# 70 small zero products on TensorE in the kernel generation, and its side jobs placed anew

## The chip, the core and the metric

The kernel runs on one core of a Trainium2 chip. A core has five engines that each take their instructions in order: TensorE (PE in the profile; its weight loads are PEld), VectorE (DVE), ScalarE (ACT), GpSimd (POOL) and SyncE (SP, which here only starts transfers). Each has its own queue, and they wait for each other by semaphores. The metric is the device time of one execution in microseconds. Of the kernel before three runs are given: median 993.96 us, from 993.62 to 994.17.

## What is computed

One block of a network with two halves, both modulated by a condition vector. The first half is a long convolution: for each of 640 channels a kernel of 2048 samples is generated from 192 complex exponentials and applied by FFT. The second is a bilinear feed-forward network. B = 1, L = 2048, D = 640, N = 192, F = 1536, all f32.

```python
logdA = dt * A;  dB = dt * Bc
P = jnp.exp(logdA[:, :, None] * l[None, None, :])
K = jnp.einsum("dn,dnl,dn->dl", Cc, P, dB).real      # the kernel sums
y = irfft(rfft(pad(u)) * rfft(pad(K)))[:L] + u * Dskip
...
mod = silu(c) @ w_mod                                 # sa, ca, ga, sb, cb, gb
h = layernorm(x) * (1 + ca) + sa
x = x + ga * conv(h)
h = layernorm(x) * (1 + cb) + sb
x = x + gb * (((h @ w_gate) * (h @ w_up)) @ w_down)
```

## The kernel before

**Generation and convolution, to about 446 us.** The 640 channels are five blocks (`db`) of 128. A block has eight kernel sums, so `n` runs from 0 to 39, and a loop of 144 turns `t` has three turns for each `n`. For one `n`, POOL multiplies out three tables (`Ph`, angles; `EQ` and `EP`, magnitudes; L710), ACT takes their sines (`trig`, into the PSUM tiles `tra`/`trb`), DVE multiplies sines and magnitudes into `QtA`, `PtA`, `QtB`, `PtB` (L765 to L792), and PE adds the products of these up in one PSUM tile `kg` (L807 and L822, 32 products each; line L811 adds the skip term). One `kg` tile serves two `n`; ACT then copies it out as `Kt`.

**Side jobs.** Everything else of the first half runs between these turns: `u_seeds` (the starting values of a block's tables, much of it DVE work in one go), `tab_ph` and `tab_eq` (table doublings on POOL), `u_k`, `u_pre`, `u_g`, `u_c`, `u_d` (the FFT of the kernel, the FFT of the input, their product and the way back, on PE, DVE and ACT; between the stages data goes through DRAM buffers such as `hm`, `FH`, `WD`), the modulation rows (L360), statistics of the inputs. `u_d` reads `WD` into a tile `TV` (L959), transforms it (L967) and adds the input (L971, L974). `row_stats` and `u_fold` stand among them too.

**What sets the order.** Nothing is scheduled at run time. The dictionary `SCHED` holds a number for each step of each side job; in turn `t` the loop runs the steps whose number, divided by 10, is `2t` or `2t + 1`, in the order of the numbers. Numbers from 2400 on come after the last kernel sum. So `SCHED` writes each engine's instruction order. `SLOT` gives, for each ring of buffers, the letter (`a`, `b`, `c`) that each new tile takes, in turn; a new tile waits until the last reader of that letter is done.

```python
def due(x):
    for _, g in sorted(jobs.pop(x, []), key=lambda j: j[0]):
        next(g, None)
```

**The passage and the second half.** After the generation the last block is transformed back. `raw` (L1000) loads raw gate weights into `wga0` and `wga1` in turn, `split_g` splits them in a high and a low part (ACT, then DVE at L1022), and `u_head` takes the statistics of the first two groups of 512 tokens (L1130), normalizes, transposes (L1160) and starts the first feed-forward products (L1197). All loads and stores of this passage that SP starts stand in one queue. `warm` adds 30 and 4 small products to a scratch tile there. From 552 us on the feed-forward network runs with its own fixed order; the change doesn't touch it.

Of the kernel before, what the change touches and what calls it, by code (L numbers as in the profile page):

```python
# [18 lines left out]
P = 128  # L19
# [9 lines left out]
TURN = float(np.float32(2.0 * math.pi / 2.0**32 * (1.0 - 1.5e-7)))  # L29

SCHED = dict(
    ml=(-885, -929, -989),
    mr=(((98, 154), (90, 130)), ((-884, 78), (-877, 73)), ((-885, -881), (-889, 132))),
    st=(
        (-955, 11),
        (-929, 195),
        (-874, 149),
        (-925, 128),
        (-938, 121),
        (-879, 152),  # L40
        (-869, 167),
        (-924, 162),
        (-995, -925),
        (-938, -871),
        (-885, 93),
        (-990, -871),
        (50, 180),
        (51, 214),
        (-930, -878),
        (-927, 39),  # L50
    ),
    hm=(
        (120, 388),
        (119, 390),
        (123, 234),
        (-949, 306),
        (-1000, 254),
        (112, 246),
        (231, 293),
        (-871, 309),  # L60
        (266, 333),
        (324, 384),
        (315, 372),
        (134, 256),
        (463, 511),
        (335, 429),
        (391, 541),
        (479, 545),
    ),
    rstd=(228, 229),  # L70
    tab=(487, 829),
    fo=(157, 189, 197, 222),
    e0=(138,),
    ds=(205, 222, 503, 397),
    mc=((-872, 289, 307, 356, 356), (217, 378, 439, 446, 461), (309, 570, 620)),
    q=(
# [4 lines left out]
    ),  # L81
    pre=(
# [5 lines left out]
    ),  # L88
    c=(
# [5 lines left out]
    ),  # L95
    d=(
# [5 lines left out]
    ),  # L102
    k=(
        (189, 202),
        (208, 226),
        (356, 358),
        (499, 559),
        (422, 496),
        (634, 660),
        (663, 672),  # L110
        (698, 713),
        (672, 682),
        (820, 837),
        (947, 972),
        (1036, 1059),
        (915, 955),
        (956, 984),
        (1080, 1094),
        (1072, 1079),
        (1271, 1275),  # L120
        (1209, 1209),
        (1528, 1540),
        (1546, 1546),
        (1406, 1429),
        (1384, 1393),
        (1533, 1569),
        (1521, 1521),
        (1684, 1715),
        (1706, 1716),
        (1931, 1933),  # L130
        (1939, 1951),
        (1911, 1915),
        (2069, 2083),
        (2033, 2056),
        (1997, 2004),
        (2286, 2306),
        (2108, 2128),
        (2368, 2376),
        (2349, 2373),
        (2504, 2534),  # L140
        (2413, 2437),
        (2492, 2495),
        (2495, 2507),
    ),
    low=((145, 411, 641, 885, 1122, 1398, 1592, 1847, 2073), (209, 434, 680, 929, 1150, 1398, 1612, 1868, 2112)),
    w=(2508, 2575, 2790, 2776, 2819, 2829),
    wl=(2444, 2450),
    wm=(2801, 2834),
    h=(2480, 2716, 2875, 2876, 2878, 2878, 2878, 2878),
    g=(  # L150
# [5 lines left out]
    ),  # L156
)

SLOT = dict(
    Kt="abababaababbbabaabab",  # L160
    Ph="abababababababababababababababababababab",
    PtA="abababababababababababababababababababab",
    TV="ababbabaababababababababababaabbaabaaababababa",
    W="abbababababababababababab",
    f16="abababa",
    gh="abcaacbabcbcbcbacbacabccabcacbabcabc",
    hf="abcabcabcabcabcabcacabcabcacacacabababacacbcbabacbacbababcbcabcab",
    psf="abcabbaaccacbabcabacbcbcabcababcbcacabcaaabcbcabcaacacacabcabcabcacbcbacbacbaacbacbacbacbbacbaccbacbacbacbaacbacbaccacab"
    "cacabcabcabccabcabcabcabcabacbacbacbacbacbacbcabcababccabcabcaabcabcabcabcabcabccabcabcabcabcabcabcabcabccacbacbbabcabca"
    "bcacabcabcabcabcabcabcabcabcabc",  # L170
    tr="abababababababababababababababababababababababababababababababababababababababababababababababababababababababababababab"
    "a",
    xs="ababababababababbbab",
)
SEG0 = ("l", "a", "b", "c", "ud", "r", "x", "e", "f", "G", "g", "D", "h", "v", "R", "")
SEG = ("l", "a", "b", "c", "ud", "D", "r", "R", "x", "eE", "f", "g", "h", "v")
# [48 lines left out]
def tile_kernel(ctx: ExitStack, tc: tile.TileContext, I, out):  # L225
    nc = tc.nc
    V, S, G, PE, SY = nc.vector, nc.scalar, nc.gpsimd, nc.tensor, nc.sync
# [15 lines left out]
    ident = const.tile([P, P], F32, name="ident")  # L243
# [26 lines left out]
    def need(n, *k):  # L270

        assert done.get(k, 0) >= n, k
# [17 lines left out]
    f16 = fft.enter_context(tc.tile_pool(name="f16", bufs=2, side="right"))  # L290
# [7 lines left out]
    ct = kconst.tile([P, 800], F32, name="ct")  # L298
# [497 lines left out]
    kg_of = {}  # L796
# [118 lines left out]
    def u_c(db, qd, parts=1):  # L915

        k0, dn = 8 * qd, P // parts
        for d0 in range(0, P, dn):
# [354 lines left out]
    at(T0["fo"], u_fold)  # L1273
    at(T0["e0"], once(lambda: LATE.pop()()))
    for j in range(4):
# [570 lines left out]
```

## Time and profile before

| | us |
|---|---|
| median of three runs (lowest, highest) | 993.96 (993.62, 994.17) |
| the profiled execution | 996.15 |
| its span, first to last instruction | 994.4 |
| its mean granted TensorE clock | 0.95 |
| PE, DVE, ACT, POOL busy in the span | 893.7, 729.1, 577.0, 510.8 |
| generation and convolution | 24 to 446 |
| passage | 446 to 552 |
| feed-forward network | 552 to 994 |

How to read the rows that the prediction quotes. A row of stretches has: from and to, length, busy time and count of PE, PEld, DVE, ACT and POOL, the clock granted to TensorE (1.00 is full), the busy share of the DMA engines, GB/s. A row of the timeline has start, length, engine, line, operation, output and inputs, tile, shape and count, and in brackets the idle time before it and what ended it. An f32 product appears as two rows on PE, so "x10" are five products and "x64" are 32. A row of waits names the engine and the line that waited, the instruction that ended it, the total, how often, and the longest. The chain of waits is followed back from the last instruction; asked for a stretch, it gives the shares by line.

### The profile page before, as it was taken

The page shows a single profiled execution, that of the slowest core. Times are in us where ns is not written, and L with a number is a line of the kernel's source. Part 1 is how long each engine was busy: PE and PEld are TensorE (multiplying, and loading weights), DVE is VectorE, ACT ScalarE, POOL GpSimd, SP SyncE. Part 2 cuts the span into 40 slices and gives each one's busy share as a digit, 9 for nine tenths or more (in the row PEclk, how much of TensorE's full clock was granted, in tenths as well). Part 3 has the DMA queues.
Part 4 walks back from the last instruction along what each step waited for, and adds up shares of the span by engine and source line. Part 5 has one row for each costly group of instructions (what it writes and reads, how often), then busy time and mean ns, then how long its engine had stood idle before and what let it go on. Part 6 is the DMA issues. An engine that isn't in the chain of part 4 may idle for free.

```text
span 994.4 us, 26747 instructions
## 1 busy us (share of the span) xinstructions
PE 893.7 (90%) x11120; PEld 725.3 (73%) x11120; DVE 729.1 (73%) x1408; ACT 577.0 (58%) x1071; POOL 510.8 (51%) x400
## 2 busy tenths in 40 slices
PE   4867898899889689998877999999999999999998
PEld 3565656676576567777635888889999788888998
DVE  8798569889989887894758655566677656568952
ACT  4869989886978878772345333334455443435430
POOL 5978899799779989950030254440113122222110
PEclk9877889899889889999999899999999999999999
DMA  8728654555246443667685565724564577658875
GB/s 262 257 54 303 219 186 136 177 167 173 77 153 194 138 123 121 188 214 236 208 230 202 172 214 187 238 92 147 155 241 114 193 228 236 217 181 290 238 239 186
DMA packets 159337, 188.54 MB, mean 190 GB/s; under 512 B 10352, under 2 KB 128880, under 8 KB 158064
## 3 DMA queue, kind: packets, MB, share of 16 engines
q1 hardware_dynamic: 150000, 155.51, 48.8%
q0 software_dynamic: 4752, 21.63, 7.5%
q10 hardware_dynamic: 4464, 9.70, 2.6%
q8 instruction: 87, 1.43, 0.6%
q14 instruction: 34, 0.28, 0.1%
HBM read 124.22 MB, written 62.59 MB: 188 GB/s over the span
## 4 chain that ended last, share of the span: by engine, by line
PE 55%; DVE 14%; ACT 12%; issue 10%; DMA 6%; POOL 2%; SPq 1%; DVEq 0%; POOLq 0%; ACTq 0%
PE pa L1074 17%; PE pa L1508 9%; PE psg L1074 8%; PE psfc L889 2%; PE kg L822 2%; PE kg L807 2%; PE psfa L889 2%; ACT L230 1%; PE psfb L889 1%; ACT trb L230 1%; DMA TVa<-WD 1%; PE psfb L946 1%; PE pa L1560 1%; ACT tra L230 1%; PE psfc L946 1%
## 5 line engine op out<-in xcount | busy, mean ns | idle before, releaser
L1051 POOL TENSOR_TENSOR tf<-wur,wgb 128x256 f32<-128x256 f32 x23 | 18.2, 792 | 251.7 <-DVE wtl L1022 204.5
L710 POOL TENSOR_TENSOR EQ<-LQ,RH 128x1536 f32<-128x1536 f32 x40 | 124.2, 3105 | 9.8 <-DVE QtB L767 9.6
L1022 DVE TENSOR_TENSOR wtl<-tf,wth 128x256 fp32r<-128x256 f32 (+1 forms) x72 | 36.6, 509 | 58.9 <-ACT wth L230 58.9
L710 POOL TENSOR_TENSOR Phb<-LH,DH 128x1536 int32<-128x1536 int32 x20 | 62.3, 3114 | 13.5 <-ACT tra L230 13.5
L710 POOL TENSOR_TENSOR EP<-LP,RH 128x768 f32<-128x768 f32 x40 | 66.0, 1651 | 0.0
L710 POOL TENSOR_TENSOR Pha<-LH,DH 128x1536 int32<-128x1536 int32 (+1 forms) x21 | 62.4, 2971 | 2.9 <-ACT trb L230 2.6
L1508 PE MATMUL pa<-wsg,sh 128*128 128x384 f32 (+1 forms) x304 | 58.6, 311 | 0.0
L822 PE MATMUL kg<-QtB,PtB 64*32 64x64 f32 x2560 | 48.5, 229 | 5.9 <-DVE QtB L766 5.3
L822 PEld LDWEIGHTS kg<-QtB,PtB 64*32 64x32 f32 x2560 | 41.5, 114 | 16.0 <-issue 7.1
L1508 PEld LDWEIGHTS pa<-wsg,sh 128*128 128x128 f32 x304 | 45.8, 189 | 0.0
L1547 POOL DMA_DIRECT2D wsg<-wdc x21 | 11.2, 532 | 66.5 <-PE pa L1560 35.5
L1022 DVE TENSOR_TENSOR wsg<-wga,wsg 128x640 fp32r<-128x640 f32 x36 | 32.9, 920 | 11.9 <-ACT wsg L230 11.9
L1074 PE MATMUL pa<-sh,wth 128*128 128x512 f32 x112 | 35.3, 397 | 6.5 <-DVE a L1423 6.1
L1022 DVE TENSOR_TENSOR sl<-a,sh 128x512 fp32r<-128x512 f32 x53 | 36.7, 712 | 5.8 <-ACT sh L230 5.8
L230 ACT ACTIVATE sh<-a 128x512 fp32r<-128x512 f32 x53 | 32.0, 622 | 14.9 <-PE psg L1560 6.2
L230 ACT ACTIVATE a<-pa 128x512 f32<-128x512 f32 x12 | 7.2, 597 | 54.7 <-PE pa L1074 54.7
L230 ACT ACTIVATE wsg<-wga 128x640 fp32r<-128x640 f32 x36 | 26.1, 729 | 21.7 <-PE pa L1508 11.0
L230 ACT ACTIVATE wth<-tf 128x256 fp32r<-128x256 f32 (+1 forms) x72 | 32.2, 479 | 9.8 <-PE pa L1074 5.3
L1074 PE MATMUL pa<-hh,wsg 128*128 128x512 f32 x136 | 36.7, 395 | 0.5 <-DVE wsg L1022 0.5
L1139 POOL TENSOR_SCALAR hfa<-xb,hr,hr 128x128 f32<-128x128 f32 x4 | 2.3, 572 | 67.6 <-DVE hr L283 67.6
L230 ACT ACTIVATE s<-pa 128x512 f32<-128x512 f32 x11 | 6.6, 598 | 49.4 <-PE pa L1074 49.4
L765 DVE TENSOR_TENSOR QtA<-tra,EQ 128x1024 f32<-128x1024 f32 x20 | 24.4, 1221 | 14.8 <-PE kg L807 9.2
(665 smaller groups left out, 3143.8 us busy)
## 6 DMA issues: line engine op xcount, KB each, us to landing
wsg<-wdc POOLq DMA_DIRECT2D x21, 640.0 KB, 5.1
wgb<-B_w_gate SPq DMA_DIRECT2D x24, 320.0 KB, 4.7
wur<-B_w_up SPq DMA_DIRECT2D x24, 320.0 KB, 6.0
wsd<-wsg SPq DMA_DIRECT2D x12, 640.0 KB, 3.9
wga<-wdg SPq DMA_DIRECT2D x12, 640.0 KB, 4.6
wsg<-wsd POOLq DMA_DIRECT2D x12, 640.0 KB, 4.7
wdc<-xb SPq DMA_DIRECT2D x21, 320.0 KB, 4.2
TVb<-WD SPq DMA_DIRECT2D x22, 256.0 KB, 3.5
```

Source lines behind the costliest of these rows:

```text
L230: return S.activation(o, i, f, **kw)
L710: G.tensor_tensor(o.rearrange("p x (h l) -> p x h l", l=8), lo.unsqueeze(2).to_broadcast([P, rows, nh, 8]), hi.rearrange("p h x -> p x h") ...
L765: return [lambda: V.tensor_tensor(Qt[:, :, :, 0:32], tr[:, :, :, ::-1], e[:, :, 0:32].unsqueeze(1).to_broadcast([P, 2, R, 32]), op=OP.mult ...
L807: PE.matmul(kg[j * 32 : j * 32 + 32, dd, :], PtA[:, c, dl * 4 + j, :], QtA[:, c, dl * 4 + j, :], start=dd == 0 and c == 0, stop=False, til ...
L822: PE.matmul(kg[j * 32 : j * 32 + 32, dd, :], PtB[lo : lo + 64, c, r, :], QtB[lo : lo + 64, c, r, :], start=False, stop=dd == 7 and c == 1, ...
L889: PE.matmul(r[c][par * 64 : par * 64 + 64, i, :], t_tw[:, k0 + k, c, :], src[:, k, :], start=True, stop=True, tile_position=(0, par * 64))
L946: PE.matmul(r[par][:, i], t_ti[lo : lo + 64, qd * 4 + i, c, :], x[lo : lo + 64, c, i, :], start=c == 0, stop=c == 1, tile_position=(lo, 0))
L1022: V.tensor_tensor(lo, v, hi, op=OP.subtract)
L1051: E.tensor_tensor(t[:, 0:2], u[:, 0:2], g[:, 0:2], op=OP.subtract)
L1074: PE.matmul(ps, w[a][:, k], x[b][:, l], start=first and n == 0 and m == 0, stop=n == 2 and m == len(ks) - 1, skip_group_check=True)
L1508: PE.matmul(AC[tb][t][c], x[:, ts], w[:, cs], start=st, stop=f == NF - 1 and n == 2 and (c == 0 or t % 2 == 1))
L1547: G.dma_start(WD[q], wdc[:, q // 3, q % 3])
```

## The change

A new job `fill` puts two products on PE. Its weights are a 64x64 corner of the identity beside the diagonal, all zeros, its moving operand 64 rows of 256 columns of a table; the result, zeros, is added to columns of the newest `kg` tile. It is called at 70 places, set by a new list `fl` in `SCHED`. All other numbers of `SCHED` in the generation and passage and the letters of `SLOT` are different too; the loop and the jobs are not. Beside the 140 products on PE, ACT has four more loads of function tables (28 for 24); DVE, POOL and SP have as many instructions as before. Of these tables a line or two is shown.

```diff
 SCHED = dict(
+    fl=(
+        358,
+        189,
...
+        2282,
+        1873,
+    ),
-    ml=(-885, -929, -989),
+    ml=(-887, -915, -977),
...
-    w=(2508, 2575, 2790, 2776, 2819, 2829),
+    w=(2453, 2558, 2624, 2678, 2865, 2688),
...
-    h=(2480, 2716, 2875, 2876, 2878, 2878, 2878, 2878),
+    h=(2626, 2738, 2749, 2789, 2845, 2851, 2863, 2877),
...
 SLOT = dict(
-    Kt="abababaababbbabaabab",
+    Kt="abaabababaababababab",
...
+    def fill():
+
+        for _ in range(2):
+            PE.matmul(kg_of[max(kg_of)][0:64, 0:4], ident[0:64, 64:P], ct[0:64, 0:256].rearrange("p (d m) -> p d m", m=64), start=False, stop=False)
+
...
+    for v in T0["fl"]:
+        at((v,), once(fill))
```

Four places in the order of the instructions. A row has line, operation, output and inputs, shape and count; the lines of the changed kernel are 77 higher (84 after `fill`), so L822 is L899, L889 is L966, L1022 is L1099.

PE before, at the burst of seeds for the last block (340 us in the profile): two kernel sums with a transform between, then the transform of an input.

```order
L526 MATMUL psfa<-ct,prm 128x8x16
L527 MATMUL psfa<-ct,prm 64x8x8
L528 MATMUL psfa<-ct,prm 64x8x8
L807 MATMUL kg<-QtA,PtAa 32x64 x32
L967 MATMUL psfb<-TVb,ct 32x512 x4
L822 MATMUL kg<-QtB,PtB 32x64 x32
L889 MATMUL psfa<-ghb,t_tw 64x128 x2
L889 MATMUL psfb<-ghb,t_tw 64x128 x2
```

PE now, at the burst of seeds for the last block; L1314 are the new products.

```order
L884 MATMUL kg<-QtA,PtAa 32x64 x32
L1314 MATMUL kg<-ct,ident 64x256 x6
L603 MATMUL psfc<-ct,prm 128x8x16
L604 MATMUL psfc<-ct,prm 64x8x8
L605 MATMUL psfc<-ct,prm 64x8x8
L603 MATMUL psfc<-ct,prm 128x8x16
L604 MATMUL psfc<-ct,prm 64x8x8
L605 MATMUL psfc<-ct,prm 64x8x8
L899 MATMUL kg<-QtB,PtB 32x64 x32
L1314 MATMUL kg<-ct,ident 64x256 x14
L966 MATMUL psfa<-f16b,t_tw 64x128 x2
L966 MATMUL psfc<-f16b,t_tw 64x128 x2
```

Six zero products stand ahead of the seeds' small products and fourteen ahead of a transform, each behind a kernel sum; a transform of the kernel follows in place of one of the input. Over the whole program the new products stand at 43 places: 29 of two, 9 of four, 3 of six and 2 of fourteen products.

ACT before, at the square roots of the row statistics (`ry<-rv`): both stand side by side.

```order
L230 ACTIVATE f16b<-psfb 128x32x16
L230 ACT_TABLE_LOAD
L230 ACTIVATE ry<-rv 128x6
L230 ACTIVATE ry<-rv 128x10
L230 ACTIVATE f16a<-f16a,nm_95,rs_94 128x640
L230 ACTIVATE PtAa<-Pha 128x1024
L230 ACT_TABLE_LOAD
```

ACT now, at the first of the two.

```order
L307 ACTIVATE TVa<-psfa 1x384
L307 ACT_TABLE_LOAD
L307 ACTIVATE ry<-rv 128x6
L307 ACT_TABLE_LOAD
L307 ACTIVATE tra<-Pha 128x512
```

The second one stands further on, with a table load of its own ahead of it and one behind.

DVE before, in the passage (484 us in the profile): the last product of transforms, the statistics, the low parts of the gate weights, then the last additions.

```order
L936 TENSOR_TENSOR f16a<-TVa,psfc 128x4x64
L1130 BN_STATS a_7256<-xb_6905 128x6 x16
L1130 BN_STATS a_7257<-xb_6906 128x6 x16
L1022 TENSOR_TENSOR wsg<-wga_7039,wsg 128x640 x2
L1022 TENSOR_TENSOR wsg<-wga_7120,wsg 128x640 x2
L974 TENSOR_TENSOR xsa<-psfb,xsa 128x512
L971 TENSOR_TENSOR xb_6905<-psfc,xsb 128x4x128
```

DVE now, at the same point of the passage.

```order
L1013 TENSOR_TENSOR f16a<-TVb,psfa 128x4x64
L1099 TENSOR_TENSOR wsg<-wga_7089,wsg 128x640
L1099 TENSOR_TENSOR wsg<-wga_7207,wsg 128x640
L1051 TENSOR_TENSOR xsb<-psfc,xsb 128x512
L1051 TENSOR_TENSOR xsa<-psfc,xsa 128x512
L1207 BN_STATS a_7499<-xb_7045 128x6 x16
L1207 BN_STATS a_7500<-xb_7046 128x6 x16
L1048 TENSOR_TENSOR xb_7045<-psfb,xsb 128x4x128
```

The low parts stand ahead of the 32 statistics, and so does one more addition; one low part has moved up among the transforms and one further back.

SP now, in the passage: the load of raw weights into the buffer that the low parts free, and behind it the loads of the transformed data. Before, the same load stood directly ahead of the load of `TVa`.

```order
L1036 DMA TVa<-WD 128x4x128 x2
L1038 DMA xsa<-A_u 128x4x128
L1077 DMA wga_7412<-B_w_gate 128x5x256
L1052 DMA x2d<-xsb 128x4x128
L1036 DMA TVb<-WD 128x4x128 x2
```

A store of a sum stands between the two now.

More of the change, by code (lines that the diff above doesn't have):

```diff
@@ L31 @@
 SCHED = dict(
-    ml=(-885, -929, -989),
-    mr=(((98, 154), (90, 130)), ((-884, 78), (-877, 73)), ((-885, -881), (-889, 132))),
-    st=(
[L35 to L50, printed above, removed]
-    ),
-    hm=(
[L53 to L68, printed above, removed]
-    ),
@@ L70 @@
[L70 to L75, printed above, removed]
-    q=(
[4 rows of a table removed]
+    fl=(
+        358,
+        189,
+        377,
+        347,
+        553,
+        317,
+        309,
+        784,
+        132,
+        90,
+        718,
+        803,
+        432,
+        709,
+        791,
+        353,
+        306,
+        370,
+        668,
+        364,
+        1281,
+        116,
+        341,
+        1157,
+        127,
+        1334,
+        1625,
+        2252,
+        1781,
+        1301,
+        2146,
+        792,
+        801,
+        2052,
+        1779,
+        326,
+        1291,
+        2052,
+        1312,
+        327,
+        1638,
+        576,
+        112,
+        1793,
+        1278,
+        1332,
+        835,
+        1766,
+        1914,
+        1558,
+        2133,
+        1765,
+        1045,
+        1269,
+        1809,
+        357,
+        1629,
+        1674,
+        1742,
+        1743,
+        1806,
+        1786,
+        1750,
+        371,
+        1785,
+        2359,
+        1773,
+        1322,
+        2282,
+        1873,
+    ),
@@ new lines @@
+    ml=(-887, -915, -977),
+    mr=(((102, 122), (102, 109)), ((-863, 86), (-886, 53)), ((-887, -872), (-887, 27))),
+    st=(
+        (-1001, 0),
+        (-975, 121),
+        (-895, 54),
+        (-993, 48),
+        (-921, 45),
+        (-906, 63),
+        (-862, 97),
+        (-870, 79),
+        (-1007, -958),
+        (-989, -919),
+        (-899, 16),
+        (-930, -867),
+        (9, 117),
+        (118, 138),
+        (-1004, -933),
+        (-947, 2),
+    ),
+    hm=(
+        (7, 398),
+        (124, 443),
+        (129, 145),
+        (-910, 267),
+        (-871, 187),
+        (146, 162),
+        (231, 259),
+        (-875, 316),
+        (287, 339),
+        (315, 380),
+        (341, 376),
+        (104, 236),
+        (470, 515),
+        (421, 468),
+        (486, 543),
+        (425, 549),
+    ),
@@ L81 @@
+    rstd=(122, 193),
+    tab=(664, 769),
+    fo=(192, 199, 221, 259),
+    e0=(66,),
+    ds=(385, 254, 475, 495),
+    mc=((-862, 143, 202, 317, 364), (195, 454, 514, 529, 549), (323, 406, 412)),
+    q=(
[4 rows of a table added]
     ),
     pre=(
[5 rows of a table removed]
-    ),
-    c=(
[5 rows of a table removed]
-    ),
-    d=(
[5 rows of a table removed]
-    ),
-    k=(
[L104 to L143, printed above, removed]
-    ),
@@ L145 @@
-    low=((145, 411, 641, 885, 1122, 1398, 1592, 1847, 2073), (209, 434, 680, 929, 1150, 1398, 1612, 1868, 2112)),
-    w=(2508, 2575, 2790, 2776, 2819, 2829),
-    wl=(2444, 2450),
-    wm=(2801, 2834),
-    h=(2480, 2716, 2875, 2876, 2878, 2878, 2878, 2878),
-    g=(
[5 rows of a table removed]
[5 rows of a table added]
+    ),
+    c=(
[4 rows of a table added]
+        (
+            (2342, 2573, 2595, 2608, 2609, 2672),
+            (2434, 2461, 2569, 2576, 2602, 2667),
+            (2604, 2630, 2645, 2646, 2690, 2696),
+            (2431, 2536, 2539, 2562, 2579, 2649),
+        ),
+    ),
@@ new lines @@
+    d=(
[5 rows of a table added]
+    ),
+    k=(
+        (186, 190),
+        (188, 193),
+        (473, 493),
+        (530, 563),
+        (415, 431),
+        (481, 530),
+        (617, 625),
+        (686, 705),
+        (641, 668),
+        (690, 716),
+        (789, 826),
+        (839, 878),
+        (895, 901),
+        (941, 961),
+        (1058, 1076),
+        (1042, 1062),
+        (1411, 1423),
+        (1353, 1371),
+        (1245, 1265),
+        (1287, 1308),
+        (1475, 1497),
+        (1398, 1418),
+        (1545, 1573),
+        (1516, 1522),
+        (1661, 1666),
+        (1735, 1736),
+        (1814, 1836),
+        (1905, 1914),
+        (1847, 1862),
+        (2005, 2007),
+        (2010, 2016),
+        (1976, 1989),
+        (2139, 2171),
+        (2106, 2112),
+        (2304, 2324),
+        (2242, 2251),
+        (2450, 2511),
+        (2320, 2330),
+        (2447, 2503),
+        (2480, 2536),
+    ),
@@ L156 @@
+    low=((143, 433, 676, 914, 1138, 1371, 1597, 1876, 2098), (213, 427, 690, 891, 1165, 1364, 1602, 1852, 2114)),
+    w=(2453, 2558, 2624, 2678, 2865, 2688),
+    wl=(2453, 2532),
+    wm=(2706, 2789),
+    h=(2626, 2738, 2749, 2789, 2845, 2851, 2863, 2877),
+    g=(
[5 rows of a table added]
     ),
@@ L159 @@
 SLOT = dict(
-    Kt="abababaababbbabaabab",
+    f16="abababa",
+    TV="ababbabababbababababaabababababbbaaababbababab",
+    gh="abcabcbacacaacabcbacacbabcacbcaacbac",
+    psf="abcabbacbacbcacaabcbcbabcabcabcabacacbabacbacbacbacccababababcababcabcabcabcabcaabcabacbacbbacbacbacbacbacbacbacbacbbcbc"
+    "abcabcabcabcabbcabcabcabcabcabacbacacbabcbcabccabacacacbcabcabcccabcabbcabcabcabcabcaabcababcabcabbcabcabbcacacacabcabca"
+    "bcabcacbabacbacbacbacbacbacbaca",
     Ph="abababababababababababababababababababab",
-    PtA="abababababababababababababababababababab",
-    TV="ababbabaababababababababababaabbaabaaababababa",
     W="abbababababababababababab",
[L165 to L170, printed above, removed]
     tr="abababababababababababababababababababababababababababababababababababababababababababababababababababababababababababab"
     "a",
-    xs="ababababababababbbab",
+    PtA="abababababababababababababababababababab",
+    Kt="abaabababaababababab",
+    hf="abcabcbcababcbcabcabcacababcabcababacacbcbcbcacacacacacacacabcabc",
+    xs="abababababababababab",
 )
```

47 rows, old and new, of tables (c, d, g, pre) are left out of this document.

## The prediction

> **What bounds the kernel now.** I read the page from the top, then three stages, then the granted clock and the chain of waits inside the first stage.
>
> ```profile
> span 994.4 us, 26747 instructions
> PE 893.7 (90%) x11120; PEld 725.3 (73%) x11120; DVE 729.1 (73%) x1408; ACT 577.0 (58%) x1071; POOL 510.8 (51%) x400
> ...
> PEclk9877889899889889999999899999999999999999
> ...
> PE 55%; DVE 14%; ACT 12%; issue 10%; DMA 6%; POOL 2%; SPq 1%; DVEq 0%; POOLq 0%; ACTq 0%
> ...
> 24.00:446.00 422.00, 361.94 (x7812) 270.15 (x7814) 355.50 (x633) 349.94 (x639) 371.89 (x222) 0.89 0.54 169
> 446.00:552.00 106.00, 84.20 (x961) 60.80 (x954) 71.54 (x180) 43.11 (x81) 9.26 (x15) 0.97 0.70 220
> 552.00:994.40 442.40, 437.53 (x2316) 387.04 (x2315) 282.02 (x511) 171.92 (x328) 117.23 (x138) 1.00 0.61 198
> ```
>
> The last three rows give, for each stage, the busy time of PE, PEld, DVE, ACT and POOL, then the granted clock. From 552 us PE is busy 437.5 of 442.4 us at full clock: that stage has nothing for this change and moves as one block. In the generation (24 to 446 us) no engine is full, four are near it: PE 362, DVE 356, ACT 350, POOL 372 of 422 us. PE stands idle there 422 − 361.9 = 60 us, and its clock is 0.89. The clock comes in whole stretches of one half, thirteen of them:
>
> ```profile
> 36.71:43.54 6.83, 6.28 (x74) 5.18 (x75) 6.79 (x14) 5.02 (x8) 6.83 (x4) 0.50 0.59 206
> ...
> 343.91:354.15 10.24, 4.87 (x72) 4.18 (x76) 10.07 (x17) 10.18 (x26) 4.29 (x3) 0.50 0.30 89
> sum 92.14, PE 76.39 PEld 61.47 DVE 75.17 ACT 80.01 POOL 70.93; mean PE 5.88 PEld 4.73 DVE 5.78 ACT 6.15 POOL 5.46
> ...
> 125.46:128.87 3.41, 2.43 (x20) 0.59 (x16) 2.14 (x5) 3.38 (x7) 3.41 (x2) 1.00 0.94 331
> 128.87:132.28 3.41, 3.41 (x72) 1.70 (x65) 0.00 (x0) 3.38 (x6) 3.41 (x2) 0.50 0.79 259
> ...
> 340.50:343.91 3.41, 0.00 (x0) 0.00 (x0) 3.41 (x10) 3.33 (x6) 3.41 (x2) 1.00 0.97 271
> 343.91:347.32 3.41, 0.00 (x0) 0.00 (x0) 3.41 (x6) 3.40 (x11) 2.52 (x2) 0.50 0.63 185
> ```
>
> 92 us pass at half clock, 76 of them with PE busy. The lower rows are neighbouring windows of 3.41 us: after one with PE busy only 2.43 us, and after one with PE wholly idle, the next runs at 0.50. What half clock does to a product, and what the added products should cost, stands in four groups (start, length):
>
> ```profile
> 114.30 2.42 PE L360 MATMUL psfb<-t_tw,sil 128*128 128x256 f32 x10
> 116.66 1.10 PE L822 MATMUL kg<-QtB,PtB 64*32 64x64 f32 x64
> ...
> 109.18 1.10 PE L822 MATMUL kg<-QtB,PtB 64*32 64x64 f32 x64
> ...
> 132.31 1.93 PE L822 MATMUL kg<-QtB,PtB 64*32 64x64 f32 x64
> ```
>
> The same kernel sum takes 1.10 us warm and 1.93 us in the stretch at 128.87.
>
> **Term 1, the clock.** Only cold PE time on the chain can shorten the run. The chain of waits, asked for single stretches, gives shares by line (a piece that crosses an edge counts whole, so a row can pass 100%):
>
> ```profile
> by line: PE psfc L360 65.6%; PE kg L822 30.0%; DVE QtB L765 10.0%; DVE QtB L766 5.0%; issue 0.6%
> ...
> by line: PE kg L807 27.3%; PE kg L822 27.3%; PE psfb L424 25.5%; PE psfc L868 25.3%; PE psfa L868 0.7%
> ...
> by line: PE psfc L889 54.8%; PE psfa L889 37.5%; PE kg L807 13.5%
> ...
> by line: PE psfa L889 57.9%; PE psfc L889 37.5%; ACT hfc L230 14.5%; PE kg L807 6.0%; issue 1.3%
> ...
> by line: PE psfa L844 57.2%; PE psfb L889 25.0%; PE psfc L889 23.8%
> ...
> by line: PE psfb L946 53.4%; PE psfb L868 21.9%; PE kg L822 17.6%; PE psfc L946 11.9%; PE psfa L868 0.8%
> ...
> by line: DVE st L473 19.6%; PE kg L822 13.6%; PE psfc L403 12.5%; PE psfb L403 5.8%; issue 5.4%; DVE mv L474 5.0%; DVE PtB L792 4.7%; DVE QtB L765 4.4%; PE psfb L404 3.1%; PE psfb L844 3.0%; DVE psfb L550 2.8%; DVE pta L549 2.7%; DVE prm L5
> ...
> by line: DMA xsb<-A_u 36.7%; PE psfb L889 19.3%; PE psfa L889 12.5%; DVE QtA L765 11.9%; DVE RH L591 11.4%; DVE PtAb L772 11.1%; PE kg L807 9.7%; DVE xsa L974 5.9%; DVE QtA L766 5.8%; DVE QtA L767 5.8%; DVE RL L589 3.6%; DVE psfc L601 2.6%;
> ```
>
> In order these are the stretches at 36.71 (6.8 us), 128.87 (6.8), 190.31 (3.4), 261.99 (3.4), 289.30 (3.4) and 320.02 (6.8): 30.6 us, and PE holds nearly all of it. The last two rows are the stretches at 53.78 (13.7 us) and 343.91 (10.2 us): PE has 38% and 41% there, 5.2 + 4.2 = 9 us, which I leave as margin. The stretches at 91.32, 173.24, 251.75 and 272.23 have their chain on ACT or DVE, in the bursts that prepare the next block's seeds. A warm PE buys nothing inside them.
>
> The first stretch follows kernel sum 0 directly, and the first added products come only behind that sum, so it stays: 30.6 − 6.8 = 23.8 us can be met, plus the margin. At full clock half goes: 12 us, 16 with the margin. ACT and DVE stand at 83% and 84% over the stage, so what PE gives up, they take in part. Bounds: 0 (they take all) and −16 us. I take −8, half of the upper end, since the chain in these rows is PE alone but its neighbours have only a sixth of slack.
>
> **Term 2, the added products.** 70 jobs of 2 products, each 256 f32 columns. L360's five products of 256 columns start at 114.30 and L822 follows at 116.66: 0.47 us a product, 0.94 us a job, 66 us in all, twice that cold. A low bound is L822's 32 products in 1.02 us, which share the array four abreast: 0.13 us for 256 columns. No row shows these alone with 64x64 weights; I take 0.47, the row with the same columns and type and no neighbour beside it. Nothing stalls them: past the first, which needs a table loaded long before, they wait for no other engine. So they run directly behind the product ahead, and cost the path only what outlasts the wait that they were put in. The cover is PE's 60 us of idle, plus 38 us that open when 76 cold busy us turn warm. Two waits show its grain:
>
> ```profile
> PE psfa L889 <- issue: 7.9, 1, 7.9
> ...
> PE psfc L868 <- ACT f16b L230: 0.7, 1, 0.7
> ```
>
> The groups of 14 products (6.6 us) fit such a wait as the first. But 29 of the 43 places hold one job, 0.94 us, against waits like the second. Behind them stand kernel sums and transforms, and for these wait DVE (the next QtA and TV) and ACT (the copies out of PSUM). If each overhangs by 0.4 us and a third of that is on the path, that is 29 × 0.4 / 3 = 4 us. Bounds: 0 and 66. I take +4.
>
> **Term 3, the order before the feed-forward stage.** The two order pieces on DVE show 32 statistics ahead of the splits of weights before, and the splits ahead now. What that costs today:
>
> ```profile
> 484.17 6.28 DVE L1130 BATCH_NORM_STATS2 a<-xb 128x6 f32<-128x128 f32 x32
> 490.37 3.01 DVE L1022 TENSOR_TENSOR wsg<-wga,wsg 128x640 fp32r<-128x640 f32 x4
> ...
> 487.57 0.33 ACTq L951 DMA_DIRECT2D WD<-Wb  x1
> ...
> 491.93 0.37 SPq L1000 DMA_DIRECT2D wga<-B_w_gate  x1
> 492.47 0.95 SPq L959 DMA_DIRECT2D TVa<-WD  x2
> ```
>
> SP's load of raw weights waits for a buffer that the second split frees, and behind it in SP's queue stands the load of TVa that the chain runs through. The last write of WD was issued at 487.57; then the DMA engines carry nothing for 2.9 us (the share 0.00 behind the clock in the row below), until the load goes at 492.5:
>
> ```profile
> 489.90:492.80 2.90, 2.90 (x15) 2.40 (x14) 2.90 (x7) 0.71 (x1) 0.00 (x0) 1.00 0.00 0
> ```
>
> That gap can close. I take −3 (bounds: 0, if the statistics, now behind, delay the next addition; −5).
>
> **Term 4, table loads.** ACT loads a table of functions when the function changes. The order now holds 28 such loads against 24, and the ACT pieces show where two of them come from: the square roots of the two row statistics no longer stand side by side. The other two come with the seeds of blocks 2 and 3, whose functions are taken in another sequence.
>
> ```profile
> L230 ACT ACT_TABLE_LOAD x24 | 30.8, 1283 | 4.8 <-DMA pta<-A_A_re 4.5
> ...
> 91.92 1.28 ACT L230
> 93.20 0.01 issue
> ```
>
> Four loads of 1.28 us are 5.1 us more on ACT. The last rows are from the chain of waits in the seed burst at 91 us, where a load lies on the path at its full length; elsewhere ACT's idle sixth can hide it. Bounds 0 and 5.1; I take +2, as part of them stand at seeds.
>
> **Everything else moved** (seeds, table doublings, statistics, transforms, the letters of the ring buffers) changes which of four nearly full engines runs late. The work is the same, so I put 0, between −5 and +10. POOL's largest stall of the kind, 11.1 us in two pieces at POOL's L650, waits for DVE's seed burst; in the new order POOL doubles another table first, which needs a result of the same burst.
>
> **Sum.** −8 + 4 − 3 + 2 = −5 us. The profiled execution took 996.15 us (span 994.4 and 1.75 around it): 991.15. It lies 2.2 us over the median of the three runs, 993.96, so the forecast is 989.
>
> **A rule against the change.** By the rows at 125.46, a window with PE 71% busy is followed by half clock. The Trainium skill, "TensorE: Matmul & The Clock Gate", section "HAM oscillation — how this bites in real kernels", puts the abstract rule as no idle gaps over about 3.4 us. By that rule short fillings do nothing in windows that had no such gap, and only the stretch after the wholly idle window would go. Those rows disagree with it; it remains as the rival below.
>
> **Rivals.**
> - *The fillings land on the path* (slower). The mechanism is Term 2 with shorter waits than now: products that start late shift, a job of 0.94 us meets a wait of 0.5, and kernel sums, PSUM copies and QtA follow late. It decides when over (8 + 3 − 2) / 66 = 14% of the added time is on the path. At a quarter, 16 us: 996.15 − 9 + 16 − 2.2 = 1001. For it speaks that most of PE's named waits are short; against it, the 98 us of cover.
> - *The gain is handed on* (same). The stretches turn warm, but the same ACT and DVE work ends the waits: clock −2, fillings +3, order −3, tables +2: 994. Speaks for it: 350 and 356 of 422 us busy.
> - *All of it arrives* (faster still): −16, +1, −3 and no table load on the path: 976.
> - *The clock doesn't answer*, because only idle windows count or because these products are too little work: fillings +4, order −3, tables +2, at most 2 us from the stretch at 343.91: 995.
>
> **Chances.** About 0.2% (2 us) is what runs of this kernel tell from no change. Forecast (984 to 992, all of it faster) 0.40; fillings on the path 0.30; gain handed on 0.15, of it 0.04 faster, 0.08 same, 0.03 slower; all arrives 0.08; no answer 0.07, of it 0.01, 0.02 and 0.04. Faster: 0.40 + 0.04 + 0.08 + 0.01 = 0.53; same 0.10; slower 0.30 + 0.03 + 0.04 = 0.37. The range 977 to 1003 leaves out half of the best case (0.04) and somewhat over a third of the fillings' case (0.12), in which a share above a quarter is on the path.
>
> **What the changed kernel's profile would show.** Right: clock of 0.95 or more over the generation, under half of the 92 cold us left, kernel sums at 1.10 us where they took 1.93, the generation's end 4 us or more before 446, and TVa's last load straight behind WD's write. Wrong: fillings on the chain of waits with more than 11 us; DVE or ACT waiting for kernel sums longer than now; cold stretches where the fillings stand. A moved step that starves POOL would undo the forecast without any of these.

## The result, and the profile after

The changed kernel took 1033.89 us (median of four runs, 1029.09 to 1045.37) against 994.07 us before: a ratio of 1.038, interval 1.034 to 1.042. The forecast was 989 us, faster by half a per cent, with a range of 977 to 1003. It is slower by 3.8%, outside the range and on the other side. Ratios here and below leave out executions disturbed by a lower clock (the 1045.37 us here and two of the four in the second experiment among them), while medians and ranges hold all.

The page of the changed kernel:

```profile
span 1032.4 us, 27305 instructions
PE 955.4 (93%) x11400; PEld 754.2 (73%) x11400; DVE 737.0 (71%) x1408; ACT 583.4 (57%) x1075; POOL 510.8 (49%) x400
...
PEclk9886588999999999999999899999999999999999
...
L1314 PE MATMUL kg<-ct,ident 64*64 64x256 f32 x280 | 82.4, 439 | 0.0
L307 ACT ACT_TABLE_LOAD x28 | 35.9, 1283 | 5.1 <-DMA pta<-A_A_re 4.3
```

POOL's work is the same, 510.8 us. PE has 62 us more, 82.4 us busy with the 140 products of the 70 fillings (two rows each). The clock has one deep hole near the start (the 5 in its row) and is near full after it.

Where the 38 us of the span lie is seen by two cuts in time: the last table that POOL makes for a kernel sum (at 436.4 us before, 481.3 now), and the end of the last kernel sum (452.2 and 494.4). Rows of the stretches, before:

```profile
24.00:436.40 412.40, 353.32 (x7636) 262.84 (x7636) 346.00 (x618) 344.77 (x629) 371.88 (x222) 0.89 0.53 167
452.20:994.40 542.20, 515.53 (x3058) 442.80 (x3058) 352.01 (x686) 213.53 (x406) 126.49 (x153) 0.99 0.63 201
```

After:

```profile
24.00:481.30 457.30, 419.81 (x7899) 294.36 (x7897) 351.31 (x616) 350.19 (x632) 374.26 (x224) 0.90 0.49 149
494.40:1032.40 538.00, 514.36 (x3090) 443.93 (x3090) 353.17 (x686) 213.60 (x406) 125.79 (x153) 0.99 0.64 206
```

Up to POOL's last table it is 44.9 us longer; between the cuts 2.7 us and behind them 4.2 us are won back: +38.0, the difference of the spans. In the first part POOL's busy time hardly moved (371.9 and 374.3 us), so its idle time took nearly all: 40.5 us before, 83.0 now. PE's clock there is 0.90 for 0.89. POOL's waits in this part, before:

```profile
POOL Phb L710 <- ACT tra L230: 13.5, 4, 6.0
POOL DL L650 <- issue: 11.1, 2, 7.4
POOL EQ L710 <- DVE QtB L767: 9.6, 3, 6.1
POOL Pha L710 <- ACT trb L230: 2.6, 3, 1.6
```

After:

```profile
POOL LQ L781 <- DVE RL L721: 39.8, 4, 22.5
POOL Pha L787 <- ACT trb L307: 13.7, 2, 9.9
POOL EQ L787 <- DVE QtB L844: 12.8, 5, 4.5
POOL Phb L787 <- ACT tra L307: 9.5, 3, 4.1
```

POOL now waits four times for the copies of seed products (LQ), one time for 22.5 us, and once 9.9 us behind ACT. Both large waits fall before 140 us. Counting each group of 32 products (one at L807 and one at L822 before) as one kernel sum, 16 to a block and 80 in all, the 18th starts at 171.6 us, 39 us later than before, and the last one 42 us later. The timeline of the changed kernel shows how they come about:

```profile
76.11 0.37 SPq L474 DMA_DIRECT2D dgd<-dcol  x1
76.57 0.46 SPq L542 DMA_DIRECT2D gha<-A_u  x1
...
89.60 0.92 ACT L307 ACTIVATE gha<-gha,nm,rs 128x640 f32<-128x640 f32 x1 [10.33 <-DMA gha<-A_u]
...
105.60 12.21 PE L1314 MATMUL kg<-ct,ident 64*64 64x256 f32 x28
...
114.48 0.36 ACT L307 ACTIVATE pta<-pta 128x192 f32<-128x192 f32 x1
...
119.80 1.22 DVE L842 TENSOR_TENSOR QtA<-trb,EQ 128x1024 f32<-128x1024 f32 x1 [6.83 <-PE kg L884]
120.12 3.67 PE L1314 MATMUL kg<-ct,ident 64*64 64x256 f32 x8
...
134.13 0.79 PE L603 MATMUL psfc<-ct,pta 128*128 128x128 f32 x2
...
135.39 0.42 DVE L721 COPY RL<-psfc 128x96 f32<-128x96 f32 x2 [13.16 <-PE psfc L605]
...
135.78 0.36 POOL L781 COPY LQ<-RL 128x96 f32<-128x96 f32 x1 [22.49 <-DVE RL L721]
```

First, SP issues a load of x right behind the scattered store of `dcol`; it lands 13 us later, ACT waits 10.3 us for it, and PE, DVE and POOL stand still with it. Then 14 products of fillings run for 12.2 us on PE, a kernel sum behind them lets DVE wait 6.8 us, four more products follow, and the last seed product, whose input ACT had at 114.8, starts at 134.1 only. POOL waits for it.

All this PE work runs at half clock, though the products fill whole windows (rows of stretches of the changed kernel):

```profile
84.76:139.38 54.62, 46.55 (x370) 27.56 (x371) 25.09 (x49) 33.22 (x63) 20.73 (x16) 0.50 0.36 115
...
108.66:112.07 3.41, 3.41 (x10) 1.81 (x9) 3.31 (x7) 3.41 (x15) 3.41 (x2) 0.50 0.37 143
112.07:115.48 3.41, 3.41 (x10) 1.81 (x9) 0.83 (x3) 3.38 (x5) 1.22 (x1) 0.50 0.00 0
115.48:118.90 3.42, 3.42 (x50) 2.06 (x52) 0.00 (x0) 3.36 (x5) 0.00 (x0) 0.50 0.24 96
```

### The profile page after: what moved, and what is told of

Same layout as the page of the kernel before. It is cut to its first block, busy times and chain, and to the rows that moved or that the text cites. A ratio compares the mean times of both kernels' runs of the same rounds, so it can differ in the third digit from the quotient of the medians.

```text
span 1032.4 us, 27305 instructions
## 1 busy us (share of the span) xinstructions
PE 955.4 (93%) x11400; PEld 754.2 (73%) x11400; DVE 737.0 (71%) x1408; ACT 583.4 (57%) x1075; POOL 510.8 (49%) x400
## 5 line engine op out<-in xcount | busy, mean ns | idle before, releaser
L1314 PE MATMUL kg<-ct,ident 64*64 64x256 f32 x280 | 82.4, 439 | 0.0
L1099 DVE TENSOR_TENSOR wtl<-tf,wth 128x256 fp32r<-128x256 f32 (+1 forms) x72 | 36.5, 509 | 59.0 <-ACT wth L307 59.0
L1314 PEld LDWEIGHTS kg<-ct,ident 64*64 64x64 f32 x280 | 39.0, 152 | 31.5 <-issue 18.1
L899 PEld LDWEIGHTS kg<-QtB,PtB 64*32 64x32 f32 x2560 | 41.2, 114 | 14.8 <-issue 7.8
L899 PE MATMUL kg<-QtB,PtB 64*32 64x64 f32 x2560 | 48.0, 228 | 3.2 <-DVE QtB L843 3.1
L1099 DVE TENSOR_TENSOR wsg<-wga,wsg 128x640 fp32r<-128x640 f32 x36 | 33.9, 944 | 10.5 <-ACT wsg L307 10.4
L1099 DVE TENSOR_TENSOR sl<-a,sh 128x512 fp32r<-128x512 f32 x53 | 36.2, 701 | 5.8 <-ACT sh L307 5.8
L307 ACT ACT_TABLE_LOAD x28 | 35.9, 1283 | 5.1 <-DMA pta<-A_A_re 4.3
L307 ACT ACTIVATE a<-pa 128x512 f32<-128x512 f32 x12 | 7.2, 599 | 54.6 <-PE pa L1151 54.6
L842 DVE TENSOR_TENSOR QtA<-trb,EQ 128x1024 f32<-128x1024 f32 x20 | 24.4, 1220 | 18.3 <-PE kg L884 11.3
```

The lines of the kernel that those rows point to most:

```text
L307: return S.activation(o, i, f, **kw)
L842: return [lambda: V.tensor_tensor(Qt[:, :, :, 0:32], tr[:, :, :, ::-1], e[:, :, 0:32].unsqueeze(1).to_broadcast([P, 2, R, 32]), op=OP.mult ...
L899: PE.matmul(kg[j * 32 : j * 32 + 32, dd, :], PtB[lo : lo + 64, c, r, :], QtB[lo : lo + 64, c, r, :], start=False, stop=dd == 7 and c == 1, ...
L1099: V.tensor_tensor(lo, v, hi, op=OP.subtract)
L1314: PE.matmul(kg_of[max(kg_of)][0:64, 0:4], ident[0:64, 64:P], ct[0:64, 0:256].rearrange("p (d m) -> p d m", m=64), start=False, stop=False)
```

## The experiments

**Fillings or order?** Three runs. The first takes all fillings out of the changed kernel (`fl=()`).

> The changed kernel with all 70 fillings taken out, its order and buffers kept. Theory F (the fillings are on the path): the loss of 40 us goes with them; the 22.5 us in which POOL waits for a seed product behind fillings fall to about 4, and the time is 1000 us or less, 995 to 1005. Rival O (the new order costs it, above all the load of x that waits 10 us behind a scattered store): the time stays at 1025 to 1036, and the wait of ACT for that load stays at 10 us. If both count, 1005 to 1020.

1024.05 us (1018.70 to 1025.25) against 994.63: ratio 1.028 (1.023 to 1.032). Neither alone: the new order costs some 27 us without a filling, the fillings about 10 more. "New order" takes in the changed letters of `SLOT` and the four table loads; no run takes these apart. ACT's wait for the load stays (9.8 us). POOL's single wait of 22.5 us shrinks to 5.9, near the 4 expected, but the other waits for seed copies are longer (up to 10.8 us), so that their sum falls from 39.8 to 28.4 us only.

The second puts the 70 fillings, with their numbers, into the order of before.

> The kernel before with the 70 fillings at the same numbers of the schedule, its order and buffers kept. Theory F: slower by 20 to 40 us, 1015 to 1035, since the fillings numbered 341 to 377 stand among the seed steps of block 1 there too (337 to 369). Rival O: 990 to 1000.

1025.85 us (1017.75 to 1034.99): ratio 1.023 (1.017 to 1.028), about 22 us for the fillings in an order that was not laid out around them.

The third takes 14 of the 70 fillings (28 products), those numbered 306 to 377, out of the changed kernel:

```diff
-    fl=(
-        358,
-        189,
...
+    fl=(189, 553, 784, 132, 90, 718, 803, 432, 709, 791, 668, 1281, 116, 1157, 127, ...
```

> The changed kernel without the 14 fillings numbered 306 to 377, which run from 96 to 132 us in its profile; the other 56 stay. Theory F in its narrow form (these 14 alone do it, since the last product of the seeds stands behind them): 1034 less 19 to 25, so 1008 to 1015. If all fillings cost alike (0.5 us each on the path): 1034 less 7, 1027. Rival O: 1030 to 1036.

1018.85 us (1017.60 to 1023.48): ratio 1.024 (1.020 to 1.029). Against the changed kernel's 1.038 these 14 jobs, a fifth of all, cost some 14 us: the narrow form, though less than the 19 to 25 us expected. The other 56 together can't be told from nothing (1.024 with them, 1.028 without), although the mean clock was higher with them (0.953 to 0.961 for 0.935 to 0.948 without).

**Why the fillings did not raise the clock.** Two runs change only the weights of a filling: the same places, columns and count.

```diff
-PE.matmul(kg_of[max(kg_of)][0:64, 0:4], ident[0:64, 64:P], ct[0:64, 0:256]...
+PE.matmul(kg_of[max(kg_of)][0:64, 0:4], ident[0:64, 0:64], ct[0:64, 0:256]...
```

> The changed kernel; the fillings keep shape, place and number, but their weights are the identity's 64x64 corner on the diagonal, not zeros, so the kernel sums get a wrong addend. In the changed kernel the clock stays at half from 84.8 to 139.4 us although windows from 95 to 132 are full of fillings. If the zeros are why (no data moves, no activity seen): the stretch ends by about 110 us, the fillings at 105 take 6 us instead of 12, and the time falls by 10 to 25 us, to 1010 to 1024. If zeros or not makes no difference: 1029 to 1045, the same stretch at half clock.

1033.98 us (1027.86 to 1036.20), ratio 1.037 (1.032 to 1.041): no difference. The row of the stretch at half clock, 47.8 us long:

```profile
87.30:135.09 47.79, 43.22 (x364) 25.37 (x364) 21.42 (x41) 31.94 (x61) 16.74 (x7) 0.50 0.38 129
```

```diff
-PE.matmul(kg_of[max(kg_of)][0:64, 0:4], ident[0:64, 64:P], ct[0:64, 0:256]...
+PE.matmul(kg_of[max(kg_of)][:, 0:4], ident, ct[:, 0:256]...
```

> The changed kernel; each filling has 128x128 weights (the identity) in place of 64x64 zeros, with the same 256 columns, so the same time on PE but four times the array; the kernel sums get a wrong addend. If the clock goes by how much of the array works: the stretch at half clock ends by about 110 us and the time falls by 10 to 25 us, to 1010 to 1024. If it goes by something else (the wait before it, DMA, other engines): the stretch stays and the time is 1029 to 1045.

1020.72 us (1017.95 to 1022.65), ratio 1.025 (1.021 to 1.029). The stretch ends after 10.2 us (its row, and that of the stretch behind it):

```profile
86.06:96.30 10.24, 5.11 (x78) 4.10 (x79) 4.41 (x10) 7.43 (x15) 1.73 (x1) 0.50 0.51 171
96.30:140.67 44.37, 41.22 (x643) 30.86 (x642) 31.15 (x56) 40.58 (x75) 38.06 (x27) 1.00 0.58 187
```

So zeros or not doesn't matter, the share of the array does: products on a quarter of it run for 12 us at half clock and leave it there; with products on all of it the stretch is short. How short is partly a matter of where a window falls: it ended at 96.30, when 0.89 us of them had run beside a kernel sum. Windows at half clock that held half a microsecond or more of added products say the same over the whole run: all eleven in the changed kernel and twelve of the thirteen in the run with nonzero weights were followed by half clock, all four in this run by full clock. The 13 us won are about what the fillings had cost. The order's 25 us stay, at a clock of 0.95 up to POOL's last table (0.89 before), so a cold PE explains little of them.

Does the first term hold where fillings are few and in the right places? The order of before, with 24 full-array products of zeros at six places:

```diff
+    fl=(61, 1285, 1400, 1625, 1770, 1775),
...
+    fz = const.tile([P, 1], F32, name="fz")
+    V.memset(fz, 0.0)
...
+    def fill():
+
+        for _ in range(4):
+            PE.matmul(kg_of[max(kg_of)][:, 0:4], ident, fz[:, 0:1].unsqueeze(2).to_broadcast([P, 4, 64]), start=False, stop=False)
...
+    for v in T0["fl"]:
+        at((v,), once(fill))
```

> The kernel before with 24 full-array products of zeros (128x128 weights, 256 columns of a zero; 0.38 us each by the full-array run) at six places ahead of five stretches at half clock (36.7, 262.0, 289.3, 320.0 and 343.9 us; 30.6 us together). If these raise the clock and the forecast's first term holds (a warm PE on the path is worth half of its cold time): four or five stretches vanish and the time falls by 4 to 8 us, to 987 to 991. If the clock rises but ACT and DVE hold the path: 993 to 997. If the products themselves hold it up: 997 to 1003.

988.31 us (986.90 to 989.54) against 994.14: ratio 0.9925 (0.9902 to 0.9948), 5.8 us faster and ahead of both kernels. Of the 92.1 us at half clock some 65 are left.

The same with 64x64 weights:

> The kernel of the run before it in the old order (24 products of zeros at six places), with 64x64 weights in place of 128x128, and nothing else changed. If only the share of the array makes a product count for the clock: the five stretches stay at half clock and the time is 994 to 1001. If small products hold a clock that is already full (as some windows of the changed kernel suggest): some stretches vanish, 989 to 993.

989.53 us (987.24 to 993.14) against 994.76: ratio 0.9944 (0.9924 to 0.9964). Quarter-array products do it too. Before, the window ahead of the stretch at 262 us and the stretch itself:

```profile
258.58:261.99 3.41, 2.43 (x79) 1.29 (x76) 3.41 (x6) 2.41 (x6) 1.77 (x2) 1.00 0.12 49
261.99:265.40 3.41, 3.36 (x34) 2.95 (x36) 3.41 (x6) 3.37 (x5) 1.70 (x1) 0.50 0.02 7
```

With four quarter-array products (1.95 us) in that window:

```profile
259.64:263.05 3.41, 3.41 (x82) 2.02 (x76) 3.41 (x6) 2.69 (x5) 1.98 (x1) 1.00 0.32 125
263.05:266.46 3.41, 3.23 (x98) 2.87 (x98) 3.29 (x6) 3.36 (x7) 1.13 (x1) 1.00 0.00 0
```

So small products can keep a clock that is full; once it has fallen, they did not bring it back. The changed kernel holds the other half of that comparison itself: 14 of its own fillings in a row, at full clock, fill a whole window there, and the next one is at full clock too.

```profile
385.13:388.55 3.42, 3.42 (x18) 2.08 (x16) 3.42 (x6) 3.41 (x10) 2.46 (x1) 1.00 0.00 0
388.55:391.96 3.41, 2.74 (x36) 1.98 (x35) 3.41 (x8) 3.41 (x12) 0.00 (x0) 1.00 0.02 5
```

**What the new order costs without fillings.** Six runs on named places. The load that waits behind the scattered store, with the fillings in:

```diff
 hm=(
...
-        (231, 259),
+        (198, 259),
```

> The changed kernel with one load of x (number 231) moved ahead of the scattered store of dcol on SP (number 198); the fillings stay. If ACT's wait of 10.3 us for that load is on the path (PE, DVE and POOL all stand still 8 to 10 us there): 1034 less 7 to 10, so 1024 to 1027, and the wait is under 1 us. If something else is late just then: 1031 to 1036.

1041.25 us (1033.08 to 1052.74), ratio 1.046 (1.037 to 1.054). ACT's wait for the load falls from 13.6 us (two waits) to 1.1, but the 12th kernel sum comes only 4.1 us earlier than in the changed kernel (128.2 us for 132.3): PE now stands still for 4.85 us in the middle of the 8th, for which the profile names no cause. The 18th comes 8.3 us earlier, the last one 2.8, and the runs are no faster. The same without fillings:

> The new order without fillings, and the load of x (number 231 to 198) ahead of the scattered store. Without fillings ACT's wait for that load is 9.8 us, and POOL waits 9.4 us behind it. Theory D (with the load in the middle of the fillings' run its gain was eaten by the fillings that came next; alone it counts): POOL's idle falls from 70 to about 61 us and the time from 1021 to 1012. Rival (something else is late just then, or a later burst takes it back): 1018 to 1024.

1017.87 us (1017.00 to 1021.89), ratio 1.024 (1.020 to 1.027), against 1.028 without the move: at most a few us, and the intervals overlap. POOL's wait behind ACT there falls from 9.4 to 4.8 us.

The last seed steps of all four blocks earlier, without fillings (block 1 shown, the others alike):

```diff
-(62, 197, 217, 273, 288, 338, 341, 351, 363, 369, 369, 370, 382, 383),
+(62, 197, 217, 273, 288, 338, 341, 351, 363, 369, 369, 370, 371, 372),
```

> The new order without fillings, and the last seed steps of blocks 1 to 4 (the phase's transposition on PE and its copies on DVE) 5 to 26 numbers earlier, right behind the amplitude's. Theory P (POOL paces the generation, and its 28 us of waiting for those copies are lost time): its waits there fall to under 14 us, and the time from 1020 (1018 to 1025 without fillings) to 1003 to 1012. Rival: PE now waits for ACT's arctangent in front of its kernel sums, and what POOL gains is lost there: 1015 to 1025.

1020.13 us (1018.65 to 1023.54), ratio 1.024 (1.021 to 1.028). POOL's waits in this kernel:

```profile
POOL LQ L710 <- DVE RL L650: 19.8, 4, 9.2
POOL EQ L716 <- DVE QtB L773: 15.0, 5, 6.4
POOL Pha L716 <- ACT trb L236: 12.6, 2, 9.1
POOL Phb L716 <- ACT tra L236: 12.5, 6, 4.5
```

The wait for the seed copies falls from 28.4 to 19.8 us, but those for QtB and tra rise from 21.2 to 27.5: the rival. PE waits for the arctangent (4.6 us at block 1), and a good part of what POOL gains comes back at its next tables.

A transform that stands ahead of a kernel sum and waits for PSUM banks of the seeds, moved behind the sum, without fillings:

```diff
-(1792, 1799, 1875, 1893)
+(1800, 1801, 1875, 1893)
```

> The new order without fillings; one transform (numbers 1792 and 1799, now 1800 and 1801) goes behind a kernel sum on PE, and DVE's order is unchanged. Without fillings that transform stands in front of the sum from 363.7 to 376.9 us, waiting 5.9 and 3.6 us for PSUM banks that DVE's seed steps of block 4 still read. Theory B (the banks held by seed steps are what the new order costs in its last part): the sum comes 5 to 9 us earlier, POOL's idle there falls by as much, and the time falls by 4 to 9 us against the new order alone (ratio 1.0275 then), to a ratio of 1.018 to 1.024. Rival (ACT and DVE are in the seed steps anyway): 1.024 to 1.030.

1020.88 us (1018.37 to 1027.44), ratio 1.026 (1.022 to 1.030): no gain. In the timeline of this kernel the sum now waits for DVE itself:

```profile
378.09 1.93 PE L813 MATMUL kg<-QtA,PtAb 128*32 128x64 f32 x64 [8.34 <-DVE PtAb L778]
```

The three moves together, without fillings:

> The new order without fillings and with three moves together: the load of x ahead of the scattered store, the last seed steps early, the transform behind the sum. If the new order's cost of 24 us lies in these three places: 1000 to 1010 (ratio 1.006 to 1.016). If it is spread over the order: 1012 to 1020 (ratio 1.018 to 1.026).

1020.73 us (1016.97 to 1024.93), ratio 1.025 (1.022 to 1.029). Spread, or elsewhere; where it arises is read from the traces further down. The opposite test, in the order of before, puts four seed steps of block 4 nearer to the later ones:

```diff
-(1298, 1403, 1490, 1732, 1735, 1735, 1746, 1763, 1773, ...
+(1298, 1403, 1490, 1732, 1765, 1766, 1768, 1770, 1773, ...
```

> The kernel before, and only the doubling steps of the seeds of block 4 (numbers 1735, 1735, 1746, 1763) moved to 1765 to 1770, behind a product of the kernel sums, as near together with the later steps as the new order has them. Theory S (close seed steps starve POOL): POOL's idle between 339 and 365 us grows from 6 to about 14 us, and the time by 4 to 8 us, to 998 to 1003. Rival (the waits are handed round and the same work is done): 992 to 996.

996.71 us (993.97 to 998.96) against 994.14: ratio 1.002 (1.000 to 1.004). POOL's wait at that block grew from 6.0 to 8.7 us, not to 14. The direction is that of theory S, the size a third of it, and the time is hardly clear of no change.

**The passage alone.** The order of before, two numbers changed:

```diff
-    w=(2508, 2575, 2790, 2776, 2819, 2829),
+    w=(2508, 2575, 2700, 2690, 2819, 2829),
```

> The kernel before, and only the low parts of the first two weight pairs ahead of the 32 statistics (numbers 2790 and 2776 become 2700 and 2690), with the raw load behind them. The forecast's third term: the DMA gap of 2.9 us at 489.9 closes, 3 us faster, 991 (0.997). If the statistics, now later, hold the end: no change, 994.

994.55 us (991.59 to 999.41) against 995.55: ratio 0.999 (0.997 to 1.002). No gain can be told. SP's load of TVa is no longer held by the raw load ahead of it, but now waits for the writes of WD themselves (two waits in a row, 6.6 and 1.3 us):

```profile
SPq L959 <- DMA WD<-Wa: 6.6, 1, 6.6
```

It starts 4.3 us behind the issue of WD's last write (485.72 to 490.06 us), for 4.9 before (487.57 to 492.47). Of the gap, 0.6 us were to be had in this way.

## Why the prediction was wrong, step by step

**Everything else moved (0, between −5 and +10) is the step that failed most.** The new order alone costs some 27 us although the rest of the run behind the last kernel sum is shorter (542.2 us before, 535.8 in the profiled run without fillings, whose span is 1016.9). I argued that the same work in another order comes out even because four engines are nearly full. The opposite follows from it: with POOL at 372 us of work, each wait of POOL lengthens the generation, and without fillings its idle time went from 40.5 us to 70 (443.9 less 374.0, in the row below).

```profile
24.00:467.90 443.90, 362.65 (x7636) 263.80 (x7636) 354.00 (x617) 349.30 (x632) 373.97 (x223) 0.89 0.50 153
```

The prediction had named the wait (POOL's stall behind DVE's seed burst, and a doubled table that needs the same burst) and then priced it at zero; it also said that a move that starves POOL would undo the forecast. That POOL's waits are the loss is an account that closes.

When it arises shows in the traces. These are the stretches of block 0, from 24 us to the start of its last kernel sum, in the kernel before, in the run without fillings and in the changed kernel:

```profile
24.00:121.70 97.70, 76.73 (x1238) 57.56 (x1236) 75.22 (x168) 82.86 (x147) 83.25 (x52) 0.77 0.62 205
24.00:137.00 113.00, 83.33 (x1246) 60.91 (x1244) 83.12 (x166) 85.34 (x150) 85.84 (x53) 0.74 0.55 167
24.00:154.20 130.20, 112.75 (x1329) 75.70 (x1327) 81.71 (x166) 86.66 (x152) 85.82 (x54) 0.71 0.48 146
```

The last kernel sum of block 0 starts 15.3 us late without fillings and 32.5 late with them; the last one of all, 27.5 and 42.2. So over half of the order's delay and most of the changed kernel's is there by the end of block 0, and POOL's idle time in it (14.5, 27.2 and 44.4 us) makes up most of that. Without fillings another 7.5 us come in block 1 and 4.7 in the three blocks behind it.

What lengthens the waits there stays partly open. The load behind the scattered store, in block 0, can account for a few us at most. Late seed products, banks held by seeds and nearness of the seed steps were worth from nothing to some 3 us when moved one by one, hardly clear of the noise, and the three moves together no more; of these the transform and the seed steps of block 4 lie where little is lost. The other moves of block 0, the letters of `SLOT` and the table loads were not tried.

**Term 1, the clock (−8).** In the changed kernel it is about 0: 88.7 us at half clock between 24 and 482 us, against 92.1. The step that failed is that a cold stretch turns warm because products are added. The hole starts at 84.8 us, where PE, DVE and ACT stand still for the load, and from there quarter-array products did not lift it. Later they did hold the clock: behind 167 us 6.8 us at half clock are left, 41 before. But from the 18th kernel sum to the last one the changed kernel loses 3 us more, so order and fillings ate that too. Where the fillings hold the clock, the size is within the term's bounds: 5.8 and 5.2 us for six places in the order of before. The Trainium skill, "TensorE: Matmul & The Clock Gate", section "HAM oscillation — how this bites in real kernels", speaks of idle gaps over about 3.4 us; by that rule short fillings should not have saved the stretch at 262 us, ahead of which PE was 71% busy, and they did. Half of that rival fell: not only wholly idle windows count. Its other half, that these products are too little work, is what the windows at half clock showed.

**Term 2, the fillings (+4).** About 10 us in the new order (1.038 against 1.028) and 22 in the old. The price of a product was near: 0.59 us (82.4 us over 140, many at half clock), and 0.48 in the run with 24 of them in the old order (11.5 us), for 0.47. Wrong was the share on the path (4 of 66 us, as a third of 0.4 us at 29 single places): the cost sat in the places with many, above all the 14 fillings between 96 and 132 us, whose largest group I had covered with an idle of 7.9 us elsewhere. The rival "the fillings land on the path" had its point of decision at 14% of 66 us; 10 us is 15%. It was right in kind, but is a quarter of the loss; the order is the rest.

**Term 3, the passage (−3).** From the last kernel sum on the changed kernel is 4.2 us shorter, about the size forecast, but as far as the runs show that is luck: the cause that I named, the splits ahead of the statistics, gave no gain that can be told when done alone. The step that failed is that SP's queue held the load of TVa; with the raw load out of its way it waits for the writes of WD, and 0.6 us are won. What shortened the passage stays open.

**Term 4, table loads (+2).** They rose as counted, 28 for 24, 35.9 us for 30.8. What of it is on the path wasn't tried.

## What to carry to other kernels

Where several engines are each 85% busy, another order is not free: name the engine whose work is longest, price each of its waits as lost time until a run says otherwise, and look first at which block the delay arises in. Fillings for the clock belong, few and small, into windows where the clock is still full and PE idle; behind a stall that has already lowered it, small ones cost their doubled time and give nothing. A load queued behind a store of scattered single values comes late; but taking a wait away pays only if the next one isn't due just then.

## What the runs showed of the hardware that was not expected

- Holding the clock and raising it differ. 1.95 us of 64x64 products in a window of 3.41 us kept it full (259.64), and so did a window wholly filled with them (385.13), while windows wholly filled with such products at half clock were followed by half clock (108.66 to 118.90). With 128x128 weights at the same places the stretch was 10.2 us long, not 47.8 or 54.6. Zero or nonzero weights made no difference.
- A load of 320 KB issued 0.46 us behind a store of 512 single values could be used 13 us later; the median of that line's loads, from issue to landing, is 5.4.
